# Two larger local units a batch, ScalarE score masks, GpSimd low bits and a new order in an attention + SoLU kernel

## The chip, the cores and the metric

The kernel runs on one core of a Trainium2 chip. That core has five engines with queues of their own: TensorE (PE in the profile, with PEld for its weight loads), VectorE (DVE), ScalarE (ACT), GpSimd (POOL) and SyncE (SP, which here only issues DMAs). The metric is the device time of one execution in microseconds (us). Three runs of the kernel before gave 503.68, 504.58 and 505.04; their median is 504.58.

## The reference

Eight batches of eight heads of attention over 576 positions with head dimension 64, and a feed-forward layer over the 4608 resulting tokens. Heads 0 to 3 see a local window of 32 positions, heads 4 to 7 see earlier positions with the same remainder modulo 32.

```python
scores = scale * np.matmul(q, k.transpose(0, 1, 3, 2))
rel = pos[:, None] - pos[None, :]
mask_local = (rel >= 0) & (rel < stride)                                  # stride = 32
mask_strided = (rel >= 0) & (pos[None, :] % stride == pos[:, None] % stride)
masks = np.stack([mask_local if h < H // 2 else mask_strided for h in range(H)], axis=0)
scores = np.where(masks[None], scores, -1e9)
attn = np.exp(scores - np.max(scores, axis=-1, keepdims=True))
attn = attn / (np.sum(attn, axis=-1, keepdims=True) + 1e-09)
x = np.matmul(attn, v)                       # then tokens by (heads x dim) = 4608 x 512
h = x @ w_in                                 # 512 -> 1024
e = np.exp(h - np.max(h, axis=-1, keepdims=True))
solu = h * (e / (np.sum(e, axis=-1, keepdims=True) + 1e-09))
mu = np.mean(solu, axis=-1, keepdims=True)
var = np.mean((solu - mu) ** 2, axis=-1, keepdims=True)
out = ((solu - mu) / np.sqrt(var + 1e-06) * g_ln) @ w_out                  # 1024 -> 512
```

The two weight matrices come as float64: the kernel is handed them as 64-bit words.

## The kernel before

**Numbers.** Products that need more than 16 bits are made of three float16 matmuls: a value is split in a high half and a low half (high x high, high x low, low x high). So each of weights, probabilities, attention outputs and layer activations has a step on ACT that writes the high half and one on DVE that writes the remainder.

**Units.** A batch's attention is cut into five units (`UNITS`): two strided ones of 6 and 5 blocks of 54 x 54 (half 1), and three local ones of 3 blocks of 64 queries x 96 keys (half 0). A unit covers two pairs of heads, so it has 2 x 6 = 12 score tiles at most. Its steps: masks into the score banks `s_ps`; scores by TensorE (line 374); the maximum (L380, DVE); for most units subtraction (L390, DVE), exponential (L392, ACT) and sum (L393, DVE), and for the units of `BY_BLOCK` the exponential tile by tile on ACT with the sum accumulated (L385); the reciprocal (L397, L398); the division (L401, POOL); the two halves (L409 ACT, L410 DVE); a DMA transpose (L412); the product with v (L432 strided, L442 local, TensorE) into the banks `x_ps`; and its two halves (L461 ACT, L462 DVE) into the buffers `xl` and `xs`. There is one pair of score banks and one pair of value banks for all units.

**Masks.** The first six units have their masks written by TensorE: a product of a unit matrix with the mask (L369). From unit 6 on (`SEEDED`) ACT copies the mask into the score banks (L361) and TensorE adds the scores to it.

**Feed-forward.** `ff(n)` works on 128 tokens, 36 times. First layer: two halves of 12 matmuls of 512 columns (L505 to L507) into two of three banks `h_ps`; maximum, exponential, products and sums on DVE and ACT (L511 to L522); small statistics on POOL (L525 to L555); the two halves of the normalized result (L562, L563), a DMA transpose (L566; the last two blocks by parts, L570); second layer: two halves of 12 matmuls (L575 to L577) into `o_ps`, the scaling (L583) and the store (L584).

**Weights.** `decode` turns the 64-bit words into float32 on the chip: ACT makes the leading bits from the upper word (L603), DVE shifts the lower word to its top three bits (L606) and joins them to the rest (L607). Each of the eight pieces is 128 x 1024. `prep_w` does so for w_in, sums its squares by TensorE (L620, and the diagonal L624) to find a power-of-two scale, and splits it (L628, L629). `prep_o` does so for w_out; its squares are made by ACT (L639, eight of them), weighted by g on DVE (L644, L645), summed by `pow2_scale` on TensorE (L264), and the matrix is split by L651 and L652.

**Order.** `Plan.add` collects the steps with their planned length and what they read and write; `ORDER` is a list of step numbers, written out in the source, and the steps are issued in that order. Each engine works through its own steps in order, so a step that waits holds all later steps of its engine. SP's queue holds loads and transposes alike. The first layer's matmuls need the split w_in and the attention outputs of their 128 tokens; the second layer's need the split w_out and the transposed activations.

Of the kernel before, what the change touches and what calls it, by code (L numbers as in the profile page):

```python
# [37 lines left out]
NU = len(UNITS)  # L38
P_SCALE = 64.0
# [12 lines left out]
SEEDED = NU + 1  # L52
BY_BLOCK = (2, 3, 4, 7, 8, 9)
# [700 lines left out]
```

## Time and profile before

| | |
|---|---|
| median of the runs (503.68 to 505.04) | 504.58 us |
| profiled execution | 503.42 us |
| its span, first to last instruction | 501.7 us |
| TensorE busy | 464.5 us, 93% |
| VectorE busy | 353.7 us, 71% |
| ScalarE busy | 364.9 us, 73% |
| GpSimd busy | 158.3 us, 32% |
| mean granted TensorE clock | 0.952 |

A row of the groups reads: line, engine, operation, out<-in with partitions x elements and type, count | busy us, mean ns of one | idle of the engine before them and what ended it. A row of the timeline or of the chain begins with its start and its length in us. In the slices each digit stands for a fortieth of the span, in tenths.

### The profile page before, as it was taken

The numbers are of one execution on the slowest core, as the hardware profiler recorded it, in microseconds if no ns is written. First come the engines' busy times: TensorE is split into PE (matmuls) and PEld (weight loads), VectorE is DVE, ScalarE is ACT, GpSimd is POOL, SyncE is SP. The second block draws the span as 40 slices with busy tenths as digits, with TensorE's granted clock in tenths as the row PEclk, the third lists the DMA queues.
The fourth block names the chain that finished last, engine by engine and source line by source line (L and its number), as shares of the span: only waits on it lengthen the run. The fifth ranks groups of instructions, "written<-read, shape, count | busy, mean of one in ns | idle before, by whom it ended". The sixth has DMA issues, their size and how long they took to land.

```text
span 501.7 us, 12430 instructions
## 1 busy us (share of the span) xinstructions
PE 464.5 (93%) x5049; PEld 240.7 (48%) x5049; DVE 353.7 (71%) x740; ACT 364.9 (73%) x647; POOL 158.3 (32%) x312
## 2 busy tenths in 40 slices
PE   6263798999999999999999999999999999999996
PEld 5153444454554545554555554555454444444442
DVE  2999888678887687787788777787756684544440
ACT  3895999987996878787786867587667677366551
POOL 3210115371342442333244231334144116132230
PEclk8555799999999999999999999999999999999999
DMA  8999787299696689888899797629754569435443
GB/s 316 381 277 338 223 244 168 60 250 231 192 254 115 162 197 204 189 231 159 233 191 209 122 230 170 146 51 197 162 103 96 95 133 171 64 78 101 65 105 105
DMA packets 153817, 88.02 MB, mean 175 GB/s; under 512 B 139808, under 2 KB 140448, under 8 KB 153248
## 3 DMA queue, kind: packets, MB, share of 16 engines
q1 hardware_dynamic: 148576, 77.79, 68.6%
q10 hardware_dynamic: 5184, 9.44, 5.8%
q8 instruction: 39, 0.64, 0.5%
q14 instruction: 18, 0.15, 0.1%
HBM read 39.24 MB, written 9.44 MB: 97 GB/s over the span
## 4 chain that ended last, share of the span: by engine, by line
PE 73%; ACT 9%; DVE 7%; DMA 5%; POOL 3%; issue 2%; SPq 1%; ACTq 0%; DVEq 0%; POOLq 0%
PE o_ps L575 11%; PE h_ps L505 10%; PE o_ps L577 10%; PE o_ps L576 10%; PE h_ps L506 10%; PE h_ps L507 10%; PE s_ps L374 6%; DMA cc<-cc 3%; PE x_ps L442 2%; PE x_ps L432 2%; ACT t L385 2%; DMA k<-kstr 1%; DVE m L380 1%; ACT raw L515 1%; DMA raw<-vstr 1%
## 5 line engine op out<-in xcount | busy, mean ns | idle before, releaser
L575 PE MATMUL o_ps<-ohi,cc 128*128 128x512 f16 x272 | 103.4, 380 | 0.9 <-DMA cc<-cc 0.9
L577 PE MATMUL o_ps<-ohi,cc 128*128 128x512 f16 x272 | 103.1, 379 | 0.0
L576 PE MATMUL o_ps<-obuf,cc 128*128 128x512 f16 x272 | 103.1, 379 | 0.0
L401 POOL TENSOR_TENSOR t<-t,m 128x576 f32<-128x576 f32 (+2 forms) x40 | 50.2, 1258 | 89.8 <-DVE m L398 63.7
L511 DVE TENSOR_REDUCE st<-h_ps 128x1 f32<-128x512 f32 x70 | 47.5, 684 | 32.6 <-PE h_ps L507 32.6
L515 ACT ACTIVATE raw<-h_ps,st,vsc 128x512 f32<-128x512 f32 x62 | 47.9, 774 | 20.4 <-DVE st L513 19.4
L563 DVE SCALAR_TENSOR_TENSOR cc<-raw,st,cc 128x1024 f16<-128x1024 f32 (+1 forms) x38 | 46.4, 1224 | 20.9 <-ACT cc L562 20.7
L517 DVE SCALAR_TENSOR_TENSOR raw<-h_ps,raw 128x512 f32<-128x512 f32 x70 | 47.3, 684 | 18.5 <-ACT raw L515 17.9
L505 PE MATMUL h_ps<-w,xl 128*128 128x512 f16 x140 | 53.8, 384 | 0.7 <-DVE raw L517 0.7
L506 PE MATMUL h_ps<-w,xl 128*128 128x512 f16 x140 | 53.4, 381 | 0.0
L507 PE MATMUL h_ps<-w,xl 128*128 128x512 f16 x140 | 53.3, 381 | 0.0
L505 PE MATMUL h_ps<-w,xs 128*128 128x512 f16 x140 | 53.1, 379 | 0.0
L506 PE MATMUL h_ps<-w,xs 128*128 128x512 f16 x140 | 53.1, 379 | 0.0
L507 PE MATMUL h_ps<-w,xs 128*128 128x512 f16 x140 | 53.1, 379 | 0.0
L521 ACT ACTIVATE raw<-raw,st 128x1024 f32<-128x1024 f32 x36 | 41.3, 1148 | 15.6 <-DVE st L520 15.2
L380 DVE TENSOR_REDUCE m<-s_ps 128x6 f32<-128x576 f32 (+2 forms) x40 | 30.4, 761 | 29.0 <-PE s_ps L374 27.9
L562 ACT ACTIVATE cc<-raw,st 128x1024 f16<-128x1024 f32 (+1 forms) x38 | 41.7, 1099 | 11.7 <-POOL st L552 8.9
L374 PE MATMUL s_ps<-k,q 64*54 64x54 f32 (+1 forms) x1280 | 45.7, 286 | 3.4 <-DMA k<-kstr 1.7
L374 PEld LDWEIGHTS s_ps<-k,q 64*54 64x54 f32 (+1 forms) x1280 | 40.0, 201 | 14.4 <-issue 7.1
L577 PEld LDWEIGHTS <-cc 128*128 128x128 f16 x288 | 28.2, 98 | 34.5 <-DMA cc<-cc 0.6
L575 PEld LDWEIGHTS <-cc 128*128 128x128 f16 x288 | 28.1, 98 | 33.5 <-DMA cc<-cc 2.0
L576 PEld LDWEIGHTS <-cc 128*128 128x128 f16 x288 | 28.2, 98 | 29.5
(149 smaller groups left out, 826.2 us busy)
## 6 DMA issues: line engine op xcount, KB each, us to landing
out<-ob ACTq DMA_DIRECT2D x36, 256.0 KB, 3.6
q<-qstr SPq DMA_DIRECT2D x8, 594.0 KB, 5.3
k<-kstr SPq DMA_DIRECT2D x8, 594.0 KB, 5.1
q<-qloc SPq DMA_DIRECT2D x8, 576.0 KB, 6.4
k<-kloc SPq DMA_DIRECT2D x8, 576.0 KB, 6.4
raw<-w_in SPq DMA_DIRECT2D x4, 1024.0 KB, 14.4
vrs<-vstr SPq DMA_DIRECT2D x5, 768.0 KB, 8.4
vrl<-vloc SPq DMA_DIRECT2D x5, 640.0 KB, 5.7
```

Source lines behind the costliest of these rows:

```text
L374: nc.tensor.matmul(s_ps[row : row + nq, pair, i * nk : (i + 1) * nk], q_raw[half][hs, q0 : q0 + (nq - 1) * nqb + 1 : nqb], k_raw[half][hs, ...
L401: add("pool", nx * nk / 520 + 0.03, lambda: nc.gpsimd.tensor_tensor(tv, tv, sm.unsqueeze(2).broadcast_to([P, nx, nk]), op=ALU.mult), r=TM, ...
L505: nc.tensor.matmul(hv[i], xhi[cc], whi[:, cc, cols], start=(cc == 0), stop=False)
L506: nc.tensor.matmul(hv[i], xhi[cc], wlo[:, cc, cols], start=False, stop=False)
L507: nc.tensor.matmul(hv[i], xlo[cc], whi[:, cc, cols], start=False, stop=(cc == 3))
L511: add("dve", 0.69, lambda i=i: nc.vector.tensor_reduce((nm, nm2)[i], hv[i], axis=AX.X, op=ALU.max, negate=True), r=[HH[i]], w=[(ST, "nm", i)])
L515: add("act", 0.73, lambda i=i, q=q: nc.scalar.activation(e[:, parts2[i]], hv[i], AF.Exp, bias=nm, scale=hs, accum_out=q), r=[HH[i], (ST, " ...
L517: add("dve", 0.7, lambda i=i, x=x: nc.vector.scalar_tensor_tensor(u[:, parts2[i]], hv[i], 1.0, e[:, parts2[i]], op0=ALU.mult, op1=ALU.mult ...
L563: add("dve", w / 980 + 0.23, lambda cols=cols: nc.vector.scalar_tensor_tensor(c[:, 1, cols], u[:, cols], r, c[:, 0, cols], op0=ALU.mult, o ...
L575: nc.tensor.matmul(o, ct[:, cc, :], ohi[:, cc, :], start=(cc == 0), stop=False)
L576: nc.tensor.matmul(o, ct[:, cc, :], olo[:, cc, :], start=False, stop=False)
L577: nc.tensor.matmul(o, ct[:, 8 + cc, :], ohi[:, cc, :], start=False, stop=(cc == 7))
```

## The change

- Batches 1 to 7 have two local units, of 5 and 4 blocks (`LATER`), in place of three of 3. Batch 0 keeps its three. A 5-block unit's values fill both banks of `x_ps`, one pair of heads in each; a 4-block unit's fill one. The buffers for scores, probabilities and transposes are now one for each kind of unit and sized for it.
- All masks are written by ACT; the strided one is read straight from the loaded mask. TensorE's mask matmuls are gone, and two early matmuls write the score banks once.
- `BY_BLOCK` holds units 2, 3, 4, 7 and 8.
- In `decode` POOL takes the top byte of the lower word and makes the three bits of it by an addition and a product that rounds to an integer; DVE only joins them.
- The sum of squares of w_out is made by TensorE from the top halves of the decoded weights, with a diagonal, and multiplied by the sum of squares of g.
- Forty warming matmuls of 128 columns become ten of 480, and the sums of squares of v go to a buffer of v's halves.
- `ORDER` is a new list of 1517 steps (1586 before).

```diff
+LATER = [(1, 0, 6), (1, 6, 5), (0, 0, 5), (0, 5, 4)]
-SEEDED = NU + 1
-BY_BLOCK = (2, 3, 4, 7, 8, 9)
+BY_BLOCK = (2, 3, 4, 7, 8)
...
-    t_sb = buf("t", [P, 12 * QS], n=NTB)
-    m_sb = buf("m", [P, 24], n=NTB + 1)
-    p_sb = buf("p", [P, 12, P], F16, n=NPB)
-    pt_sb = buf("pt", [P, 12, P], F16, n=NPT)
+    t_sb = [buf(f"t{j}", [P, w])[0] for j, w in enumerate((12 * QS, 10 * QS, 10 * KL, 8 * KL))]
+    m_sb = buf("m", [P, 24], n=5)
+    p_sb = [buf(f"p{j}", [P, w, P], F16)[0] for j, w in enumerate((12, 12, 20, 16))]
+    pt_sb = [buf(f"pt{j}", [P, w, P], F16)[0] for j, w in enumerate((20, 16))]
...
-    add("pe", 2.13, warm, r=["ones"], w=["o"])
+    add("pe", 0.4, lambda: warm(2, [s_ps[:, i, 0 : 5 * KL] for i in range(2)]), r=["ones"], w=[("s", 0), ("s", 1)])
+    add("pe", 2.0, lambda: warm(10, [o_ps[:, 0 : 5 * KL]]), r=["ones"], w=["o"])
+    add("dve", 0.1, lambda: nc.vector.memset(s_ps[:, 1, 504:512], 0.0), w=[("s", 1)])
...
     def unit(n):
         b, j = divmod(n, NU)
-        half, b0, nb = UNITS[j]
+        half, b0, nb = (LATER if b else UNITS)[j]
...
-        if n >= SEEDED:
-
-            def seed():
-                nc.scalar.copy(s_ps[:, :, 0 : nb * nk], mk.unsqueeze(1).broadcast_to([P, 2, nb * nk]))
-
-            add("act", nx * nk / 1200 + 0.17, seed, r=["mask"], w=[("s", 0), ("s", 1)])
+        if half:
+            mk, MK = mask_sb[:, 2:3, 0:QS].unsqueeze(1).broadcast_to([P, 2, nb, QS]), "mask_raw"
+        else:
+            mk, MK = mk_loc[:, 0 if b0 == 0 else 1, 0:nb].unsqueeze(1).broadcast_to([P, 2, nb, KL]), "mask"
+        add("act", nx * nk / 1200 + 0.17, lambda: nc.scalar.copy(sv, mk), r=[MK], w=[("s", 0), ("s", 1)])
...
-            for pair, h, hs, row in heads if n < SEEDED else ():
-                nc.tensor.matmul(s_ps[row : row + D, pair, 0 : nb * nk], unit_sb[hs, hs], mk[hs], start=True, stop=False)
...
-        nt = 12
+        nt = 12 if half else 2 * nx
...
+        one = half == 0 and nb <= 4
+        X = [("x", xb)] if one else [("x", 0), ("x", 1)]
...
-        def bits():
-            nc.vector.tensor_scalar(w0, w0, 29, None, op0=ALU.logical_shift_right)
-            nc.vector.scalar_tensor_tensor(di, di, 3, w0, op0=ALU.logical_shift_left, op1=ALU.bitwise_or)
-
-        add("dve", 2.02, bits, r=[*RAW, *w], w=[*w, *RAW], lock=True)
+        top = raw.bitcast(U8).rearrange("p f (t b) -> p f t b", b=4)[:, :, 0, 3]
+        add("pool", 1.05, lambda: nc.gpsimd.tensor_scalar(w0, top, -15.5, 1.0 / 32, op0=ALU.add, op1=ALU.mult), r=RAW, w=[("low", n)])
+        add("dve", 1.25, lambda: nc.vector.scalar_tensor_tensor(di, di, 3, w0, op0=ALU.logical_shift_left, op1=ALU.bitwise_or),
+            r=[*RAW, ("low", n), *w], w=[*w, *RAW], lock=True)
...
     def prep_o():
+        add("dve", 0.2, lambda: nc.vector.scalar_tensor_tensor(gs_sb, g_sb, 1.0, g_sb, op0=ALU.mult, op1=ALU.mult, accum_out=o_sc[:, 9:10]), r=["g"], w=["gm", "gs"])
...
-            for cc in (2 * i, 2 * i + 1):
-                add("act", 0.71, lambda cc=cc: nc.scalar.activation(ob_sb[cc % 2][:, 0 : DM // 2].bitcast(BF16), obuf[:, cc], AF.Square,
-                                                                   scale=2.0**-SQ, accum_out=o_sc[:, 8 + cc : 9 + cc]),
-                    r=[("od", cc)], w=[("om", cc), ("ob", cc % 2)])
-
-        def comb():
-            nc.vector.tensor_tensor(o_sc[:, 8:16], o_sc[:, 8:16], g_sb, op=ALU.mult)
-            nc.vector.tensor_tensor(o_sc[:, 8:16], o_sc[:, 8:16], g_sb, op=ALU.mult)
+            def gram(i=i, dst=dst):
+                x = dst.bitcast(BF16).rearrange("p (f t) -> p f t", t=2)[:, :, 1]
+                for j in range(8):
+                    nc.tensor.matmul(o_ps[:, 0:P], x[:, j * P : j * P + P], x[:, j * P : j * P + P], start=(i == 0 and j == 0), stop=(i == 3 and j == 7))
+
+            add("pe", 0.6, gram, r=OD, w=["o"])
+
+        add("dve", 0.3, lambda: nc.vector.scalar_tensor_tensor(diag, o_ps[:, 0:P], 1.0, unit_sb, op0=ALU.mult, op1=ALU.mult, accum_out=o_sc[:, 8:9]),
+            r=["o", "unit"], w=["om"])
...
-        for j in range(2, NU - 1):
+        last = len(LATER if b else UNITS) - 1
+        for j in range(2, last):
```

More of the change, by code (lines that the diff above doesn't have):

```diff
@@ L221, in attn_solu_kernel, with warm @@
     add("dve", 0.3, lambda: nc.vector.memset(ones, 1.0), w=["ones"])
-    def warm():
-        for _ in range(40):
-            nc.tensor.matmul(o_ps[:, 0:P], ones, ones, start=True, stop=True)
-    add("pe", 2.13, warm, r=["ones"], w=["o"])
+    def warm(n, out):
+        for i in range(n):
+            nc.tensor.matmul(out[i % len(out)], ones, ones[:, 0:1].broadcast_to([P, 5 * KL]), start=True, stop=True)
+    add("pe", 0.4, lambda: warm(2, [s_ps[:, i, 0 : 5 * KL] for i in range(2)]), r=["ones"], w=[("s", 0), ("s", 1)])
+    add("pe", 2.0, lambda: warm(10, [o_ps[:, 0 : 5 * KL]]), r=["ones"], w=["o"])
+    add("dve", 0.1, lambda: nc.vector.memset(s_ps[:, 1, 504:512], 0.0), w=[("s", 1)])
     def masks_bf16():
         m = mask_sb
-        nc.gpsimd.tensor_copy(mk_str, m[:, 2:3, 0:QS].broadcast_to([P, 6, QS]))
         nc.gpsimd.tensor_copy(mk_loc[:, 0, 0:1], m[:, 0:1])
-        nc.gpsimd.tensor_copy(mk_loc[:, 0, 1:3], m[:, 1:2].broadcast_to([P, 2, KL]))
-        nc.gpsimd.tensor_copy(mk_loc[:, 1], m[:, 1:2].broadcast_to([P, 3, KL]))
+        nc.gpsimd.tensor_copy(mk_loc[:, 0, 1:5], m[:, 1:2].broadcast_to([P, 4, KL]))
+        nc.gpsimd.tensor_copy(mk_loc[:, 1], m[:, 1:2].broadcast_to([P, 5, KL]))
     def load_masks():
         add("sp", 0.4, lambda: nc.sync.dma_start(mask_sb, masks), w=["mask_raw"])
-        add("pool", 1.34, masks_bf16, r=["mask_raw"], w=["mask"])
-    for i in range(NPB):
+        add("pool", 1.4, masks_bf16, r=["mask_raw"], w=["mask"])
+    for i in range(4):
         def pads(i=i):
-            nc.gpsimd.memset(p_sb[i][:, :, QS:D], 0.0)
-            nc.gpsimd.memset(p_sb[i][:, :, D if i == 1 else KL : P], 0.0)
-        add("pool", 0.56, pads, w=[("p", i)])
+            if i < 2:
+                nc.gpsimd.memset(p_sb[i][:, :, QS:D], 0.0)
+            nc.gpsimd.memset(p_sb[i][:, :, (KL, D)[i == 1] : P], 0.0)
+        add("pool", (0.56, 0.9, 0.6, 0.5)[i], pads, w=[("p", i)])
     def unit_matrix():
@@ L262, in total @@
             for i, part in enumerate(parts):
-                nc.tensor.matmul(tot, ones, part.bitcast(BF16)[:, 1:2], start=(i == 0 and not adds), stop=(i == len(parts) - 1), skip_group_check=adds)
+                one = product or not (i or adds)
+                nc.tensor.matmul(tot[:, i : i + 1] if product else tot, ones, part.bitcast(BF16)[:, 1:2], start=one, stop=product or i == len(parts) - 1, skip_group_check=adds)
         add("pe", 0.06 * len(parts) + 0.05, total, r=["ones", *r], w=[T])
         def root():
-            nc.vector.tensor_scalar(dst[:, 0:1].bitcast(I32), tot.bitcast(I32), 1, 0x7F800000, op0=ALU.logical_shift_right, op1=ALU.bitwise_and)
+            low = tot
+            if product:
+                low = dst[:, 0:1]
+                nc.vector.tensor_scalar(low, tot[:, 0:1], tot[:, 1:2], None, op0=ALU.mult)
+            nc.vector.tensor_scalar(dst[:, 0:1].bitcast(I32), low.bitcast(I32), 1, 0x7F800000, op0=ALU.logical_shift_right, op1=ALU.bitwise_and)
         def fn():
@@ L278, in fn @@
                 nc.vector.tensor_scalar(dst[:, 2:3], dst[:, 1:2], dst[:, 1:2], square, op0=ALU.mult, op1=ALU.mult)
-        add("dve", 0.16, root, r=[T], w=[(w, "root")])
+        add("dve", 0.32 if product else 0.16, root, r=[T], w=[(w, "root")])
         add("dve", 0.54, fn, r=[(w, "root")], w=[w])
@@ L300, in v_scale @@
         raw = raw_v(b)
+        junk = v_sb[1][b % 2]
         for a in range(2):
             def square(a=a):
-                nc.scalar.activation(junk[:, 0 : VW[a]], vr_sb[raw][a], AF.Square, scale=2.0**-SQ, accum_out=vm[:, a : a + 1])
-            add("act", (1.36, 1.58)[a], square, r=[("vr", a, raw)], w=["junk", ("vm", b % 2, a)])
+                nc.scalar.activation(junk[:, a, 0 : VW[a]], vr_sb[raw][a], AF.Square, scale=2.0**-SQ, accum_out=vm[:, a : a + 1])
+            add("act", (1.36, 1.58)[a], square, r=[("vr", a, raw)], w=[("v", 1, b % 2, a), ("vm", b % 2, a)])
         room = (s_ps[:, 1, 512 - b : 513 - b], ("s", 1)) if b else (h_ps[2][:, 0:1], ("h", 2))
-        pow2_scale(sc, [vm[:, 0:1], vm[:, 1:2]], [("vm", b % 2, a) for a in range(2)], ("vsc", b % 4), room, 8, 1.0 / P_SCALE, adds=b > 1)
+        pow2_scale(sc, [vm[:, 0:1], vm[:, 1:2]], [("vm", b % 2, a) for a in range(2)], ("vsc", b % 4), room, 8, 1.0 / P_SCALE, adds=b > 0)
         def hscale():
@@ L374, in qk @@
                     nc.tensor.matmul(s_ps[row : row + nq, pair, i * nk : (i + 1) * nk], q_raw[half][hs, q0 : q0 + (nq - 1) * nqb + 1 : nqb],
-                                     k_raw[half][hs, k0 : k0 + nk], start=False, stop=(i == nb - 1), skip_group_check=n >= SEEDED)
-        add("pe", nb * 0.231 + (0.25, 0.09)[half] - (0.2 if n >= SEEDED else 0.0), qk, r=[("q", half), ("k", half), "mask", "unit", "kpad"], w=[("s", 0), ("s", 1)])
+                                     k_raw[half][hs, k0 : k0 + nk], start=False, stop=(i == nb - 1), skip_group_check=True)
+        add("pe", nb * 0.231 + (0.25, 0.09)[half] - 0.2, qk, r=[("q", half), ("k", half), "kpad"], w=[("s", 0), ("s", 1)])
         SS = [("s", 0), ("s", 1)]
@@ L404, in unit @@
         if half == 0:
-            hi, lo = (pb[:, 6 * a : 6 * a + 6, 0:nk] for a in range(2))
+            hi, lo = (pb[:, nx * a : nx * a + nx, 0:nk] for a in range(2))
         else:
@@ L438, in pv @@
                     vv, vb = (v_sb[0][0] if blk % 2 else ve_sb), (blk + 1) // 2
-                    for a, (vp, pp) in enumerate((vv[0:nk, a], ptb[0:nk, y + x]) for a, y in ((0, 0), (0, 6), (1, 0))):
+                    for a, (vp, pp) in enumerate((vv[0:nk, a], ptb[0:nk, y + x]) for a, y in ((0, 0), (0, nx), (1, 0))):
                         for h in range(2):
                             v0 = (vb * 4 + 2 * pair + h) * D
-                            nc.tensor.matmul(x_ps[xb][h * D : (h + 1) * D, x * nq : (x + 1) * nq], vp[:, v0 : v0 + D], pp[:, (h ^ pair) * QL : (h ^ pair) * QL + nq],
+                            nc.tensor.matmul(x_ps[xb if one else pair][h * D : (h + 1) * D, (x if one else i) * nq : ((x if one else i) + 1) * nq], vp[:, v0 : v0 + D], pp[:, (h ^ pair) * QL : (h ^ pair) * QL + nq],
                                              start=(a == 0), stop=(a == 2))
@@ L449, in unit @@
             q0, w = off + QL * b0, QL * nb
-            src = [x_ps[xb][:, 0 : 2 * w].rearrange("p (c q) -> p c q", c=2)]
-            dst = [[x[:, :, q0 : q0 + w] for x in xl]]
+            src = [x_ps[xb][:, 0 : 2 * w].rearrange("p (c q) -> p c q", c=2)] if one else [x[:, 0:w] for x in x_ps]
+            dst = [[x[:, :, q0 : q0 + w] for x in xl]] if one else [[x[:, c, q0 : q0 + w] for x in xl] for c in range(2)]
             ring = [("xl", q0 // QL + i) for i in range(nb)]
@@ L458, in unit @@
         for c, (src, (dh, dl)) in enumerate(zip(src, dst)):
-            w = 2 * by_row[c] * nq if half else nx * nq
-            K = [(*x, c) if half else x for x in ring]
+            w = 2 * by_row[c] * nq if half else (2 if one else 1) * nb * nq
+            K = [(*x, y) for x in ring for y in (range(2) if one else (c,))]
             add("act", w / 1200 + 0.17, lambda src=src, dh=dh: nc.scalar.copy(dh, src), r=[X[c]], w=[(*x, "h") for x in K])
@@ L479, in ff @@
         bs = sorted({n * P // S, (n * P + P - 1) // S})
-        ring = [("xl", pos // QL + i, a) for i in range(2) for a in "hl"]
+        ring = [("xl", pos // QL + i, c, a) for i in range(2) for c in range(2) for a in "hl"]
         ring += [("xs", b % 2, b0, c, a) for b in bs for b0 in R0 for c in range(2) for a in "hl"]
@@ L681, in attn_solu_kernel @@
                 o_factor(b + 1)
-        unit(b * NU + NU - 1)
+        unit(b * NU + last)
         if b == 0:
```

43 lines of the change are left out of this document (16 added, 27 removed), and 78 rows, old and new, of the table ORDER.

## The prediction

> **What bounds the kernel now.** I read the page's slices first. In them TensorE (PE) is thin for the first eighth of the span and full from then on; the granted clock is a half in that first part.
>
> ```profile
> PE   6263798999999999999999999999999999999996
> PEclk8555799999999999999999999999999999999999
> ```
>
> The timeline dates the change: VectorE (DVE) and ScalarE (ACT) begin near 9.3 us, the first feed-forward (ff) matmul at 55.8, the first of the second layer at 79.5.
>
> ```profile
> 9.23 1.27 ACT L303 ACTIVATE junk<-vrl 128x1280 bf16<-128x1280 f32 x1 [7.17 <-DMA vrl<-vloc]
> ...
> 55.79 0.61 PE L505 MATMUL h_ps<-w,xl 128*128 128x512 f16 x1
> ...
> 79.48 0.39 PE L575 MATMUL o_ps<-ohi,cc 128*128 128x512 f16 x1 [0.89 <-DMA cc<-cc]
> ```
>
> Then the busy time by stage. The columns are the stretch, its length, then the busy time of PE, PEld, DVE, ACT, GpSimd (POOL), then PEclk and the DMA share.
>
> ```profile
> 9.30:62.00 52.70, 25.40 (x543) 19.33 (x543) 48.78 (x88) 43.78 (x98) 7.72 (x7) 0.55 1.02 311
> 30.00:40.00 10.00, 4.98 (x136) 4.59 (x140) 9.03 (x27) 9.96 (x25) 2.26 (x3) 0.50 1.07 285
> 40.00:50.00 10.00, 3.18 (x101) 2.86 (x96) 9.37 (x9) 4.76 (x6) 1.15 (x1) 0.50 1.16 342
> 62.00:100.00 38.00, 35.12 (x367) 16.95 (x366) 30.37 (x73) 36.11 (x86) 13.64 (x27) 1.00 0.64 161
> 100.00:498.00 398.00, 397.58 (x4051) 198.71 (x4049) 274.28 (x578) 282.99 (x463) 133.09 (x264) 1.00 0.73 157
> ```
>
> So there are two kernels in one. Up to 62 us DVE sets the pace: 48.8 of 52.7 us busy, against 43.8 for ACT, a PE that mostly waits, and an idle POOL. From 62 to 100 PE is nearly full and ACT too (36.1 of 38). After 100 us PE sets it alone: 0.4 us of 398 idle, DVE at 69%, ACT at 71%. Work taken off DVE counts in the first part; in the second only what shortens PE's own stream counts. The chain of waits shows the same: before 62 us it runs through DVE's decoding of the weights, later through PE steps without a gap.
>
> ```profile
> 48.17 0.61 DVE raw L606
> ...
> 48.87 1.24 DVE obuf L607
> ...
> 50.13 0.72 ACT ob L639 x2
> ```
>
> **The change, startup part.** These are the groups of the first 64 us that it touches.
>
> ```profile
> L606 DVE TENSOR_SCALAR raw<-raw 128x1024 int32<-128x1024 int32 x7 | 4.8, 685 | 0.0
> L624 DVE SCALAR_TENSOR_TENSOR diag<-h_ps,unit 128x128 bf16<-128x128 f32 x1 | 0.3, 292 | 0.5 <-PE h_ps L620 0.5
> L639 ACT ACTIVATE ob<-obuf 128x512 bf16<-128x512 f32 x8 | 5.0, 627 | 3.9 <-DVE obuf L607 3.8
> L361 ACT CAST s_ps<-mk_loc 128x576 f32<-128x576 bf16 x1 | 0.6, 639 | 0.0
> L620 PE MATMUL h_ps<-cc 128*128 128x128 bf16 x32 | 4.1, 305 | 3.3 <-DVE cc L607 3.3
> L232 POOL CAST mk_loc<-mask 128x96 bf16<-128x96 f32 x1 | 0.3, 270 | 0.0
> L234 POOL CAST mk_loc<-mask 128x288 bf16<-128x288 f32 x1 | 0.4, 432 | 0.0
> L401 POOL TENSOR_TENSOR t<-t,m 128x576 f32<-128x576 f32 (+2 forms) x7 | 8.5, 1227 | 47.9 <-DVE m L398 28.6 <-ACT xl L461 14.3 <-DVE o_sc L644 5.0
> ```
>
> *DVE.* Eight shifts of L606 (seven in this group, one on the other staging tile) leave it: 8 x 0.685 = -5.5 us. Two small products (L644, L645) go, and a small operation in the root and the squares of g come: they cancel. New is a diagonal like L624 with the read of its accumulator: +0.4. In batch 1 three local units become two. A reduction of the same kind took 0.828 us for 648 elements and 0.715 for 540, so 1.05 ns an element:
>
> ```profile
> L380 DVE TENSOR_REDUCE m<-s_ps 128x12 f32<-128x648 f32 x8 | 6.6, 828 | 10.9 <-PE s_ps L374 10.9
> L380 DVE TENSOR_REDUCE m<-s_ps 128x10 f32<-128x540 f32 x8 | 5.7, 715 | 1.5 <-PE s_ps L374 1.5
> L380 DVE TENSOR_REDUCE m<-s_ps 128x6 f32<-128x576 f32 x24 | 18.1, 754 | 16.6 <-PE s_ps L374 15.5 <-ACT raw L521 1.1
> L397 DVE TENSOR_SCALAR m<-m 128x6 f32<-128x6 f32 x24 | 4.7, 195 | 0.1
> ```
>
> By that slope units of 960 and 768 elements take 1.16 + 0.96 instead of 3 x 0.754, -0.14 for the maximum and as much for the low half, and three small operations of one unit, 0.19 each like L397, go: -0.9. In sum DVE loses 6.0 us before the first second-layer matmul.
>
> *ACT.* Eight squares go, 0.72 each in the chain above (two of them, cut, in the row; 0.63 plus the accumulator's read in the group): -5.8. Six units that PE seeded with the masks are now seeded by ACT: one of 0.71, one of 0.61, three of 0.64 and one of 0.71, scaled from L361: +4.0. Net -1.9. ACT had 8.9 us idle between 9.3 and 62, so with a window 6.0 shorter and 1.9 less work it keeps 4.8. It also begins earlier: its first operation waited until 9.23 for v, which the new order loads ahead of q and k. So it is no bound, but nearly one.
>
> *POOL.* It gets the eight masks, as one operation with one input of 1024 elements. The casts give 0.84 ns an element over 0.19 us, so 1.05 us; from above, L401 with two inputs gives 1.227/576 = 2.13 ns, 2.2 us. I take 1.05, the row with one input. POOL was idle for 45 of these 53 us, so its own time hides. Behind each mask on POOL's queue stands the next unit's L401; a mask that waits for its weights' DMA would hold that too, but weights 0 are loaded before the local q and k in the new order.
>
> The Trainium skill, GPSIMD Engine Reference, 4.1 Engine selection, says one-input elementwise work there is roughly at line rate; an estimate from its 1.03 cycles an element at 1.2 GHz is 0.88 us plus dispatch, and the term would not change by it.
>
> What does not hide is that POOL and DVE get in each other's way. The same operation of DVE, with two inputs from SBUF, took 1.80 us at 19.09 and 2.38 at 40.38, where it met an L401:
>
> ```profile
> 19.09 1.80 DVE L326 SCALAR_TENSOR_TENSOR vs<-vrs,vsc,vs 128x1536 f16<-128x1536 f32 x1
> ...
> 40.00 1.15 POOL L401 TENSOR_TENSOR t<-t,m 128x576 f32<-128x576 f32 x1 [7.02 <-DVE m L398]
> 40.38 2.38 DVE L326 SCALAR_TENSOR_TENSOR vs<-vrs,vsc,vs 128x1536 f16<-128x1536 f32 x1 [0.55 <-ACT vs L325]
> ```
>
> The overlap was 0.77 us and DVE lost 0.58. Half of DVE's startup work is of that kind (L326, L410, L607, L629). If every second mask meets it for half its length, 8 x 0.5 x 0.5 x 0.58/0.77 = 1.5; part of this is a wait that L606 would have caused as DVE work. I charge +1.0, with 0 and 8.4 (all masks waited out) as ends.
>
> The Trainium skill, SBUF — State Buffer, section "SBUF: two separate sides", states it harder: the pair of ports is an exclusive lock and the loser blocks for the whole instruction. By it the 40.38 operation would have ended at 41.15 + 1.80 = 42.95; it ended at 42.76, so the trace nearly agrees, and a DVE that always lost would pay 8.4 us, which is the slower rival below.
>
> *PE and order.* The sums of squares of w_out add 32 matmuls like L620, four groups of 1.03 us at half clock, 0.5 at full. Two groups now stand behind the first ff half, in PE's queue ahead of the second: +1.0. The 24 mask matmuls (L369) go, off the path. The new order loads v first and q, k after: DVE's first large operation comes near 11.5 us instead of 9.26, but the scaling of v, some 2.5 us of DVE, is then already done; I count zero. The DMA share is 1.16 at 40 to 50 us, and w_out waits for staging rooms as before: +1.0 for that and for ACT, with 0 and 4 as ends. Startup: -6.0 + 1.0 + 1.0 + 1.0 = -3.0 us; ends -6 and +5.
>
> **The change, PE-bound part.** All ff matmuls stay. What changes is how often PE is interrupted by attention. The chain gives each such visit; a steady ff step is 0.22, the step after a visit 0.32:
>
> ```profile
> 126.70 0.22 PE h_ps L506
> ...
> 145.56 1.18 PE s_ps L374 x40
> ...
> 155.40 0.88 PE s_ps L374 x24
> ...
> 158.98 0.69 PE x_ps L442 x36
> 159.66 0.32 PE o_ps L575
> ...
> 164.95 1.26 PE x_ps L442 x72
> ...
> 186.36 0.70 PE x_ps L432 x72
> ...
> 189.76 1.39 PE s_ps L374 x48
> 191.15 0.32 PE h_ps L505
> ...
> 283.16 0.70 PE x_ps L432 x72
> 283.86 1.34 PE s_ps L374 x48
> 285.20 0.32 PE h_ps L505
> ```
>
> A lone local unit costs 0.88 + 0.10 for its scores and 0.69 + 0.10 for its values. Scores of 40 and 48 matmuls differ by 0.21, 0.026 a matmul; on that slope 40 and 32 local ones cost 1.30 + 1.09 + 0.20 = 2.59 against 3 x 0.98 = 2.94, -0.35. Were all of 0.88 proportional, 1.47 + 1.17 + 0.20, only -0.10. Values: 36 more matmuls cost 0.57, so 60 and 48 take 1.07 + 0.88 + 0.20 = 2.15 against 2.37: -0.22. A batch saves 0.32 to 0.57; seven batches 2.2 to 4.0; I take 3.1. Visits joined save a switch: the pair at 283.16 cost 0.70 + 1.34 + 0.10 = 2.14, the two alone 0.80 + 1.49 = 2.29, so 0.15. After the first second-layer matmul the old order has 57 visits with 14 joints, the new one 37 with 21: 7 more, -1.0 (0 to -1.5). The small remainder of batch 1 that the new order has yet to do is +0.1. Part two: -4.0, ends -2.2 and -5.5. The rest (DVE, ACT, transposes with 20 + 16 tiles for 3 x 12) is hidden under that full PE while DVE and ACT have 30% free; without it nothing of it would exceed the 0.8 us a batch counted above, in the good direction.
>
> **Sum.** The profiled execution took 503.42 us (span 501.7 and 1.7 around it). 503.42 - 3.0 - 4.0 = 496.4. The median of the runs, 504.58, stands 1.2 above the profiled one, so 497.6.
>
> **Rivals.**
> 1. *ACT or the loads take DVE's place in the startup.* ACT's work falls by 1.9 only, and from 30 to 40 us it is busy 9.96 of 10, and from 62 on it is full; against it stand its idle half at 40 to 50 and its earlier start. Startup then gains 0 to 1.9, and the time is 504.6 - 4.0 - 1 = 499.6.
> 2. *Larger units stall PE.* One unit of 5 blocks keeps the score banks for 0.97 + 1.4 + 1.16 + 1.15 us and needs both value banks, so a score visit can find them unready. For it: the score banks exist once. Against it: PE waited 0.4 us in 398, and four large units keep the banks no longer than five small ones. At 0.6 us a batch, 7 x 0.6 = 4.2, part two is gone: 501.7.
> 3. *Slower: GpSimd and DVE exclude each other in the startup.* Place: the eight masks, each between the landing of weights and DVE's L607. Price: at 2.2 us a mask and a DVE that waits it out, 17.6 instead of the 1.0 charged: 497.6 + 16.6 = 514; with half of it covered by DVE work from PSUM, 505.4; middle 510. It decides from (504.6 - 497.6 + 1.0)/8 = 1.0 us of DVE wait a mask, the whole of my 1.05.
> 4. *No change:* part one returns nothing and the new order, with ACT full between 62 and 100, adds 3.4 us of idle PE to the 2.9 there: 504.6 - 4.0 + 3.4 = 504.
>
> **How the numbers follow.** Forecast 0.60 (493 to 501), rival 1 0.15, rival 2 0.10, rival 3 0.09, rival 4 0.06. About 0.3%, 1.5 us, is what a measurement tells from no change. Faster: 0.60 + 0.15 + 0.09 of rival 2 = 0.84; same: rival 4 and the rest of rival 2, 0.07; slower 0.09. The range runs from 504.6 - 6 - 5.5 = 493 to 503, which takes in rivals 1 and 2 and leaves rivals 3 and 4 and a tail of the forecast out.
>
> **What would show it.** Right: DVE's masks gone and POOL's about 1.05 us each; the first ff matmul near 51 us, the first second-layer one near 76.5; 37 visits after it, local scores of 40 matmuls near 1.3 us; PE from there to its end 4 us shorter. Wrong: POOL masks over 2 us and L607, L629 or L410 stretched beside them; ACT full while DVE idles before the first ff matmul; PE idle by more than 2 us after 100 us with a release by s_ps seeds or x_ps copies.

## Result and profile after: slower, with less work on every engine that mattered

The changed kernel takes 507.46 us (median of 12 executions, 505.43 to 510.96) against 504.96 for the kernel before in the same sessions: a ratio of 1.0053, 95% interval 1.003 to 1.0076. It was forecast at 497.6 and came out slower by 0.5%; the interval begins at the 0.3% that can be told apart. The profiled execution took 505.71 us (span 504.0), 2.3 more than that of before.

The timeline of TensorE in the changed kernel (start, duration, engine, line) has the first feed-forward (ff) matmul 1.2 us earlier than before, and the first of the second layer 2.1 us later. Line numbers are those of the changed kernel, two or three below those of before.

```profile
54.61 0.61 PE L503 MATMUL h_ps<-w,xl 128*128 128x512 f16 x1
...
81.60 0.39 PE L573 MATMUL o_ps<-ohi,cc 128*128 128x512 f16 x1 [0.22 <-DMA cc<-cc]
...
499.90 0.38 PE L575 MATMUL h_ps<-ohi,cc 128*128 128x512 f16 x1
```

Stretches of the prediction, columns as there (PE, PEld, DVE, ACT, POOL, PEclk, DMA share, and last GB/s):

```profile
9.30:62.00 52.70, 29.86 (x586) 22.17 (x586) 42.76 (x76) 39.26 (x79) 21.54 (x19) 0.64 1.04 317
62.00:100.00 38.00, 33.21 (x435) 16.98 (x434) 31.36 (x75) 35.28 (x88) 13.65 (x25) 1.00 0.78 190
100.00:498.00 398.00, 393.88 (x3994) 198.74 (x3992) 273.96 (x543) 280.12 (x444) 132.64 (x259) 1.00 0.71 153
```

VectorE lost 6.0 us of work before 62 us (48.78 to 42.76), ScalarE 4.5. That the first equals the 6.0 that was worked out is partly luck, since other steps now fall into the stretch: over the first 100 us VectorE lost 4.9 (79.44 to 74.50). The freed time stayed empty: VectorE is busy for 81% of the stretch instead of 93%. From 62 to 100 us TensorE idles 1.9 us more than before, from 100 to 498 us 3.7 us more (4.1 of 398, it was 0.4).

The cleanest account is TensorE from its first to its last ff matmul. Before:

```profile
55.79:498.02 442.23, 438.93 (x4476) 218.53 (x4472) 310.45 (x662) 324.67 (x565) 147.95 (x291) 1.00 0.72 157
```

After:

```profile
54.61:500.28 445.67, 436.56 (x4509) 220.64 (x4506) 311.09 (x626) 319.86 (x539) 148.68 (x285) 1.00 0.72 158
```

So: start -1.2, work -2.4 (438.93 to 436.56; two groups of the new sums of squares now lie in this stretch), idle +5.8 (3.30 to 9.11), together +2.3, the whole difference. The waits of TensorE in that stretch, by releaser (total us, times, longest):

```profile
PE o_ps L573 <- DMA cc<-cc: 3.1, 4, 1.8
PE h_ps L503 <- DVE raw L515: 2.2, 3, 1.5
PE o_ps L573 <- ACT s_ps L364: 1.4, 1, 1.4
PE h_ps L573 <- DMA cc<-cc: 1.2, 1, 1.2
```

The largest, 4.3 of 9.1 us, is the DMA transposition of the second layer's input (cc<-cc, median 4.7 us from issue to landing) that landed late; the 4.1 us of idle time behind 100 us are all of this kind. The row that names ScalarE's score seed (s_ps L364) may be one more: its wait ended at 94.90, and the transposition for that matmul, issued at 88.25, had landed only at 94.77. The chain of waits of the changed kernel shows three late transpositions between 100 and 480 us, two of them below, and, in the startup, three transfers that hold 23.5 us of the chain between 9 and 62 us. In the kernel before that chain ran over VectorE and ScalarE alone until 59.9.

```profile
26.78 8.05 DMA pt<-p
...
39.41 6.30 DMA raw<-w_out
...
50.21 9.15 DMA q<-qloc
...
152.48 8.03 DMA cc<-cc
...
299.84 9.66 DMA cc<-cc
```

The GpSimd operation on the low bits (L606; the prediction calls it a mask) behaves as costed where it is alone, and not where it meets VectorE. Groups of the changed kernel:

```profile
L606 POOL TENSOR_SCALAR raw<-raw 128x1024 int32<-128x1024 uint8 x7 | 10.7, 1525 | 16.0 <-DMA raw<-w_out 12.8 <-DMA raw<-w_in 3.1
L606 POOL TENSOR_SCALAR cc<-cc 128x1024 int32<-128x1024 uint8 x1 | 1.1, 1135 | 2.1 <-DVE m L379 2.1
L650 DVE TENSOR_SCALAR gs<-g,o_sc 128x8 f32<-128x8 f32 x1 | 1.6, 1603 | 0.0
```

The timeline shows whom it meets. A join of VectorE (L607, which joins the low bits to the rest) keeps its 1.22 us, and the GpSimd operation beside it takes 2.07. Later a tiny VectorE product of eight columns, 0.22 us before, takes 1.60 beside a GpSimd division that now has 960 elements.

```profile
15.07 1.22 DVE L607 SCALAR_TENSOR_TENSOR cc<-cc,raw 128x1024 int32<-128x1024 int32 x1
15.27 2.07 POOL L606 TENSOR_SCALAR raw<-raw 128x1024 int32<-128x1024 uint8 x1
...
66.49 1.79 POOL L400 TENSOR_TENSOR t<-t,m 128x960 f32<-128x960 f32 x1 [0.96 <-DVE o_sc L276]
66.71 1.60 DVE L650 TENSOR_SCALAR gs<-g,o_sc 128x8 f32<-128x8 f32 x1
```

That product gates the first scaled second-layer weight on ScalarE. The Trainium skill, SBUF — State Buffer, section "SBUF: two separate sides", says that whoever starts first holds the shared pair of ports and the other blocks for the whole instruction; both pairs of rows agree: the GpSimd operation ends 1.05 us behind the join (alone it takes 1.09 to 1.14), and the product ends within 0.03 us of the division.

### The profile page after: what moved, and what is told of

It is laid out like the page before. It is cut to its first block, busy times and chain, and to the rows that moved or that the text cites. A ratio compares the mean times of both kernels' runs of the same rounds, so it can differ in the third digit from the quotient of the medians.

```text
span 504.0 us, 12300 instructions
## 1 busy us (share of the span) xinstructions
PE 460.2 (91%) x5023; PEld 239.0 (47%) x5023; DVE 348.5 (69%) x695; ACT 359.6 (71%) x617; POOL 170.3 (34%) x312
## 4 chain that ended last, share of the span: by engine, by line
PE 71%; DMA 12%; ACT 8%; DVE 3%; issue 2%; POOL 1%; SPq 1%; ACTq 0%; POOLq 0%; DVEq 0%
PE o_ps L573 11%; PE o_ps L574 10%; PE o_ps L575 10%; PE h_ps L503 10%; PE h_ps L504 9%; PE h_ps L505 9%; PE s_ps L373 5%; DMA cc<-cc 5%; DMA pt<-p 3%; PE x_ps L440 2%; DMA q<-qloc 2%; PE x_ps L430 2%; ACT t L384 2%; DMA raw<-w_out 1%; ACT vs L307 1%
## 5 line engine op out<-in xcount | busy, mean ns | idle before, releaser
L400 POOL TENSOR_TENSOR t<-t,m 128x648 f32<-128x648 f32 (+4 forms) x33 | 47.3, 1434 | 99.7 <-DVE m L397 63.2
L561 DVE SCALAR_TENSOR_TENSOR cc<-raw,st,cc 128x1024 f16<-128x1024 f32 (+1 forms) x38 | 47.5, 1251 | 21.9 <-ACT cc L560 21.6
L373 PE MATMUL s_ps<-k,q 64*54 64x54 f32 (+1 forms) x1280 | 44.1, 284 | 12.6 <-ACT s_ps L364 12.4
L373 PEld LDWEIGHTS s_ps<-k,q 64*54 64x54 f32 (+1 forms) x1280 | 38.9, 201 | 20.9 <-ACT s_ps L364 15.5
L581 ACT ACTIVATE ob<-o_ps,st 128x512 f32<-128x512 f32 x34 | 23.3, 684 | 30.1 <-PE o_ps L575 15.9
```

The source lines that it names most:

```text
L373: nc.tensor.matmul(s_ps[row : row + nq, pair, i * nk : (i + 1) * nk], q_raw[half][hs, q0 : q0 + (nq - 1) * nqb + 1 : nqb], k_raw[half][hs, ...
L400: add("pool", nx * nk / 520 + 0.03, lambda: nc.gpsimd.tensor_tensor(tv, tv, sm.unsqueeze(2).broadcast_to([P, nx, nk]), op=ALU.mult), r=TM, ...
L561: add("dve", w / 980 + 0.23, lambda cols=cols: nc.vector.scalar_tensor_tensor(c[:, 1, cols], u[:, cols], r, c[:, 0, cols], op0=ALU.mult, o ...
```

## Experiments

Five readings of these profiles were set against each other. *Theory 1*: the startup is bound by the DMA engines (98.8% busy in the first 60 us before, 100.1% after), so VectorE's saving buys nothing. *Theory 2*: GpSimd and VectorE exclude each other, so the operations themselves give the gain back. *Theory 3*: the saving of VectorE is real and only the new order brings transfers into the chain. *Theory 4*, formed from the account of TensorE: the operations are worth what was predicted, and the complete order that came with them loses it again by idle TensorE; *theory 5* is its rival, that such gaps only show where the engines are late, and come back elsewhere.

### One part alone: low bits on GpSimd in the kernel before

```diff
-            nc.vector.tensor_scalar(w0, w0, 29, None, op0=ALU.logical_shift_right)
+        # in the step of the Prelu:
+            nc.gpsimd.tensor_scalar(w0, top, -15.5, 1.0 / 32, op0=ALU.add, op1=ALU.mult)
```

> The kernel before, its order unchanged, with only the low three bits of the weights moved to GpSimd (the shift of L606 becomes a GpSimd operation on the top byte, issued right behind the Prelu). Prediction's step: DVE bounds the startup, so eight shifts of 0.62 to 0.68 us less bring -4.5 us (498.5 to 501 on the median), first second-layer matmul near 75. Theory 1 (the DMA engines, busy 98.8% of 0 to 60 us, bound the startup under any order): -1 to 0 us, that matmul within 1 us of 79.5. Theory 2 (GpSimd and VectorE exclude each other, so the moved work comes back as waits): 0 to +2 us, the GpSimd operation at 1.8 us and more where a two-input VectorE operation runs. Theory 3 (only the new order brings the transfers into the chain, the DVE saving is real): -3 to -5 us.

Measured: 506.46 us, ratio 1.0032 (1.0017 to 1.0047), slower; the first second-layer matmul came at 82.25. VectorE's busy time in the startup fell by 1.5 us only, from 48.78, although 5.5 us of shifts are gone (lines of this run's own kernel):

```profile
9.30:62.00 52.70, 23.55 (x505) 17.59 (x500) 47.30 (x75) 42.48 (x92) 20.94 (x14) 0.74 0.99 310
```

The rest went into longer operations. The four joins of w_in take 1.68 us each where they took 1.23, as the group shows,

```profile
L612 DVE SCALAR_TENSOR_TENSOR cc<-cc,raw 128x1024 int32<-128x1024 int32 x4 | 6.6, 1682 | 0.0
```

and in the timeline two low halves (L410) of 576 elements take 1.64 to 1.66 where they took 0.75:

```profile
46.67 1.20 POOL L607 TENSOR_SCALAR raw<-raw 128x1024 int32<-128x1024 uint8 x1 [0.85 <-DMA raw<-w_out]
46.82 1.66 DVE L410 TENSOR_TENSOR p<-t,p 128x576 f16<-128x576 f32 x1
...
50.57 1.21 POOL L607 TENSOR_SCALAR cc<-cc 128x1024 int32<-128x1024 uint8 x1 [2.71 <-PE s_ps L374]
50.73 1.64 DVE L410 TENSOR_TENSOR p<-t,p 128x576 f16<-128x576 f32 x1
```

So theory 2 describes this kernel. Under an order not made for it the moved work comes back as longer operations: of the 5.5 us taken away, VectorE's busy time in this stretch kept 4.0, 1.8 of it in the four joins and 1.8 in the two low halves. Theory 3 as stated falls.

### The same part undone in the changed kernel

```diff
-        add("pool", 1.05, lambda: nc.gpsimd.tensor_scalar(w0, top, -15.5, 1.0 / 32, ...), ...)
+        add("pool", 1.05, lambda: None, r=RAW, w=[("low", n)])
+            nc.vector.tensor_scalar(w0, w0, 29, None, op0=ALU.logical_shift_right)   # ahead of the join
```

> The changed kernel with its own order, low three bits back on VectorE (shift and join, as before). Prediction's step: +4.5 us. Theory 1 and theory 3 (in the changed kernel the chain of 0 to 62 us runs over transfers, VectorE has room): 0 to +1.5 us, first second-layer matmul 81.6 to 83. Theory 2 (exclusion costs what was gained): -1 to -2 us.

Measured: 509.86 us, ratio 1.0099 (1.0078 to 1.012): 2.4 us above the changed kernel, first second-layer matmul at 83.33. Under the new order the low bits on GpSimd do help, by half of the 4.5 charged. (The profiled execution also ran 3.4 us at half rate near 311 us, of which below; how much of the 2.4 this is stays open.) Theory 2 alone cannot be the loss.

### Fewer bytes

```diff
-        load(1.49, q_raw[half][:, 0:w], (qloc, qstr)[half][b], [("q", half)])
+        load(1.49, q_raw[half][:, 0:w], (qloc, qstr)[half][b], [("q", half)], skip=b == 1)   # keys, values too
```

> The kernel before without the six loads of batch 1 (queries, keys and values of batch 1 are not read; batch 1 is computed from batch 0's), 3.8 MB less in the startup. Theory 1: several us faster, -3 us or more at the first second-layer matmul (79.5). Theory 3: its chain of 9 to 60 us runs over VectorE and ScalarE alone, so 0 to -1 us. Theory 2: nothing to say of it.

> The changed kernel without the six loads of batch 1 (batch 1 is computed from batch 0's queries, keys and values). Theory 1 and theory 3: its chain holds 23.5 us of transfers by 62 us, so the first second-layer matmul comes 3 to 6 us earlier than 81.6 and the time is 501 to 504. Theory 2: no change, 507.

Batch 1 is then computed from batch 0's inputs, so only the time of these runs is of use. Measured: 504.77 us without these loads in the kernel before, ratio 1.0001 (0.9991 to 1.0011); 507.63 in the changed one, 1.0046 (1.0017 to 1.0076). The first 60 us of the first move 14.9 MB instead of 18.8, and the busy share of the queue in the DMA view falls from 98.8% to

```profile
q1 hardware_dynamic: 10896, 14.84, 81.7%
```

and nothing comes earlier for it. The first second-layer matmul comes at 80.60, against 79.48 with all loads; in the changed kernel it comes at 81.50, against 81.60. Theory 1 falls in both kernels; a queue that is always busy was no bound. In the changed kernel without these loads one transposition still landed 10.69 us after its issue at 41.48; two of w_out's loads stood ahead of it.

### Repairing single places of the new order

The first run moved four steps; the lines below give one of these moves in words. A tile is a block of 128 tokens, and "two moves" are two DMA copies on the chip (ve<-vl).

```diff
-  ... load v (batch 7), two moves, transposition of tile 17 ...
+  ... transposition of tile 17, load v (batch 7), two moves ...
```

> The changed kernel with four places of its order moved and nothing else: the second-layer transposition of tile 17 goes ahead of the load and the two moves that stood in front of it in SP's queue (landing 9.66 us after its issue at 299.84, TensorE idle 1.84 us at 309.55), that of tile 6 ahead of one load (8.03 us at 152.48, idle 0.87 at 160.55), and the last tile's transpositions are issued as soon as each quarter is written (idle 1.22 at 494.92). Theory 4 (the changed kernel loses by idle TensorE between its matmuls, 9.10 us behind the first feed-forward matmul against 3.27 before, and these places are of the order, not of the new operations): the three gaps go, idle 5.5 to 7, time 3 us less, 503.5 to 505. Theory 5 (the gaps only show where the other engines are late, and come back elsewhere): 506.5 to 508, idle 8.5 or more.

Measured: 507.29 us, ratio 1.0054 (1.0036 to 1.0071), no gain. The tail's gap is gone and the wait at 160 us too, but at 310 us the gap came back longer, with another releaser: the squares of v of batch 7, one of whose loads now stands behind the transposition. In all TensorE idles 7.7 us from its first ff matmul on (9.1 in the changed kernel), between the two ranges that were expected. That first matmul came at 56.70, 2.1 us later, though nothing was moved ahead of it: so much can two profiles of one startup differ. And after 3.4 us of idleness TensorE's steps take 0.43 us instead of 0.22 until 314.7:

```profile
310.82 0.19 PE L263 MATMUL s_ps<-vm,ones 128*128 128x1 bf16 x2 [3.40 <-ACT vs L307]
...
311.69 0.63 PE L573 MATMUL o_ps<-ohi,cc 128*128 128x512 f16 x1
...
314.93 0.38 PE L575 MATMUL o_ps<-ohi,cc 128*128 128x512 f16 x1
```

The granted clock of 312 to 318 us is 0.77 there, against 1.00 in the changed kernel's own trace, where the idleness was 1.83. The Trainium skill, TensorE: Matmul & The Clock Gate, Part 1, puts the fall to half rate behind a window of about 3.4 us without work; the 3.40 us here agree, other traces of nearly the same order don't. The kernel with fewer loads fell behind 2.99 us (0.81 in the same stretch), the second run of this section behind 2.24, and the one with the low bits on VectorE behind 1.95:

```profile
310.35 0.39 PE L573 MATMUL o_ps<-ohi,cc 128*128 128x512 f16 x1 [1.95 <-DMA cc<-cc]
...
312.57 0.63 PE L575 MATMUL o_ps<-ohi,cc 128*128 128x512 f16 x1
```

The third run of this section did not fall behind 2.81 us (clock 1.00):

```profile
311.27 0.39 PE L573 MATMUL o_ps<-ohi,cc 128*128 128x512 f16 x1 [2.81 <-DMA cc<-cc]
```

So the length of one idle time does not decide it in these traces. Theory 5 holds for this place: the order around 300 us is too tight for that move.

```diff
-  ... load w_out 0, load w_out 2, a move, transposition of unit 2 ...
+  ... a move, transposition of unit 2, load w_out 0, load w_out 2 ...
```

> The changed kernel with two of the four loads of w_out issued behind the transposition of unit 2 instead of ahead of it (that transposition, issued at 41.54, landed only near 52.5, and ScalarE idled 3.16 us for it). If the order of the SP queue makes the start late: that transposition lands within 6 us, first feed-forward matmul 51 to 53 instead of 54.6. If w_out's own path to the scaled second-layer weights sets the first second-layer matmul, that one stays at 81.6 or comes up to 3 us later; if ScalarE's idle time between 50 and 62 us sets it, it comes 1 to 3 us earlier. Time 505 to 508.

Measured: 512.58 us, ratio 1.0154 (1.0128 to 1.018); first ff matmul at 59.59, five later. The sums of squares of w_out stand in TensorE's queue ahead of the scores and values that the first ff matmul needs, and they now waited for the late weights:

```profile
54.00 1.89 PE L643 MATMUL o_ps<-obuf 128*128 128x128 bf16 x16 [7.62 <-DVE obuf L607]
```

A third run moved a single step: it put the ten matmuls on ones behind the scores of unit 5, so that TensorE would be at full rate for the first ff matmuls.

> The changed kernel with one step moved: the ten matmuls on ones (at 11.74 us in its profile) go behind the scores of unit 5 (45 us). If the half rate of the first eight feed-forward matmuls (0.43 us instead of 0.2157, 54.61 to 57.57) comes from TensorE's idleness before them, they run at the full rate and the time falls by 0.5 to 2 us; if the start is bound by ScalarE behind 62 us anyway, the matmuls are faster and the time stays within 1 us of 507.

Measured: 509.44 us, 1.0093 (1.0059 to 1.0126). The first six ff matmuls still took some 0.42 us a step (55.20 to 57.71); another wait of 2.33 us stood between. The gap at 311 us was 2.81 us. It doesn't answer its question.

### The order as a whole

The next kernels keep every operation and replace only the text of ORDER. Two complete orders come from one sum: each step starts when its engine is free and what it reads is there, with the durations noted at the steps, and single steps are moved until the end is early.

```diff
 ORDER = """
-10 6 1 15 8 16 9 13 11 14 20 25 17 18 53 30 52 54 19 2 55 35 12 4 56 60 58 5 61 59 3 21 22 62 123 63 7 23 76 64 77 26 27 65 92 66 78 67 79 93 97 80 98
+(another order of the same steps)
```

> All new operations of the change under another complete order, found by moving single steps of the changed kernel's order so that the end, as worked out from the durations noted at the steps (the scores 0.225 us dearer, as the traces show), is early for early and for late transfers alike (1.9, 2.6 and 3.4 us from queue to landing). Theory 4: TensorE idle behind the first feed-forward matmul under 5 us, time 497 to 502. Theory 2 (GpSimd and VectorE exclude each other, a cost of the operations themselves): 504 or more under any order.

> The kernel before under an order found in the same way from its own. By the same sum the new operations are worth 3.7 us between the two orders so found. Theory 4: 499 to 504, so 2 to 5 us above the changed kernel's contents under their order. Theory 2: the two within 1 us, or this one faster.

Measured: 506.39 us for the new operations (1.0036, 1.0012 to 1.0061), 505.17 for the old (1.0005, 0.9994 to 1.0016). By these numbers it is theory 2's ranges that are met. But its reason isn't in the trace of the first: that one begins its ff matmuls at 50.74, 3.9 us earlier than the changed kernel and at full rate, and then loses 11 us of idle TensorE (under 5 were expected), half of it in one wait:

```profile
50.74 0.39 PE L503 MATMUL h_ps<-w,xl 128*128 128x512 f16 x1
...
95.73 0.58 PE L573 MATMUL o_ps<-ohi,cc 128*128 128x512 f16 x1 [5.26 <-DMA cc<-cc]
```

That transposition was issued at 85.33 and landed 10.27 us later, behind two other transpositions, two moves and a load. The sum had given transpositions the noted durations. So it was fitted to the first and last ff matmul of six measured kernels, with transpositions 1.5 to 1.9 times as long as noted, an issue that blocks SP while the queue is full, and 4 us of half rate after more than 2.5 us of idle TensorE. These are settings of the sum and not measurements: the idle times above do not bear out the 2.5.

> All new operations of the change under a third order. The sum behind it is fitted to six runs measured so far (first and last feed-forward matmul of each): transpositions take 1.5 to 1.9 times the noted duration in the queues, SP's issue of one blocks while the queue before it is full, TensorE runs at half rate for 4 us after more than 2.5 us of idleness. Theory 4 (order, not operations): TensorE idle behind the first feed-forward matmul under 5 us against 9.1, last matmul 491 to 495, time 496 to 500, faster than both kernels. Theory 2 (operations themselves cost the gain): 503 or more.

> All new operations of the change under a fourth order from the same fitted sum, searched from the changed kernel's own order with another seed. Theory 4: 496 to 501; a spread of more than 4 us between this and the other order of the same sum would say that the sum, not the operations, is what is short.

> The kernel before under an order from the same fitted sum. By that sum its last matmul comes 5 to 7 us behind that of the changed operations under theirs: 497 to 500, time 502 to 505. Theory 4: that difference is the worth of the operations, about what was predicted for the whole change (-7 us). Theory 2: the two within 2 us.

> The operations of the kernel before under a second order from the fitted sum (last matmul at 496.3 in the sum, against 491.3 for the new operations). If the worth of the operations is what the first pair showed (498.61 against 505.10): 502 to 506. If that pair was a lucky draw of orders: 500 or less.

| operations | order | us | ratio to before (95%) |
|---|---|---|---|
| new | fitted, first | 498.61 | 0.9878 (0.9855 to 0.990) |
| new | fitted, second | 503.68 | 0.9967 (0.9945 to 0.9988) |
| new | of the change | 507.46 | 1.0053 (1.003 to 1.0076) |
| old | of the kernel before | 504.96 | 1 |
| old | fitted, first | 505.10 | 1.0001 (0.9983 to 1.0019) |
| old | fitted, second | 506.62 | 1.0044 (1.0029 to 1.0059) |

The first is faster than both kernels, by 6.4 us against before, within 1.0 us of the forecast. Its rows: the ff matmuls begin at 48.15, 6.5 us earlier than in the changed kernel, and TensorE idles 0.35 us of the 393 behind 100 us.

```profile
48.15 0.61 PE L503 MATMUL h_ps<-w,xl 128*128 128x512 f16 x1
```

```profile
48.15:492.68 444.53, 438.09 (x4525) 221.42 (x4522) 317.37 (x635) 323.00 (x542) 161.72 (x289) 1.00 0.76 163
100.00:492.60 392.60, 392.25 (x3946) 196.51 (x3943) 271.14 (x533) 277.33 (x443) 141.24 (x264) 1.00 0.74 154
```

Against before it starts 7.6 us earlier, works 0.8 less and idles 3.1 more; 5.8 of its 6.4 us of idle time (under 5 were expected) lie before 82 us. The forecast had 3.0 for the startup and 4.0 behind it, so the nearness of the totals is partly luck. Its first second-layer matmul comes at 83.21, later than in either kernel: TensorE had other work. In its SP queue the transpositions of batch 0's first four units stand ahead of the loads of w_out:

```profile
41.16 1.62 SPq L411 DMA_TRANSPOSE pt<-p  x1
42.89 1.37 SPq L288 DMA_DIRECT2D raw<-w_out  x2
```

The median landing of its second-layer transpositions is 5.4 us, later than the 4.7 of the changed kernel, and no matmul waits for one. What differs, it seems, is the room that the order leaves them. Theory 4 is borne out: the best order of the new operations is 6 us faster than the best of the old ones, and four orders of the same operations lie 9 us apart. How much the operations are worth in general is less sure. In pairs of one search the new ones gain 6.5 us (first fitted), 2.9 (second fitted), and lose 1.2 (not fitted). The two fitted orders of the new operations are 5 us apart as well, so the sum behind them is short too; 503.68 and 506.62 lie above the ranges expected for them. One thing holds for all three searches: the first ff matmul comes at 48.15 to 50.74 with the new operations and at 56.68 to 58.04 with the old ones.

### Which operations carry it

> The fastest order so far (498.61 us with the new operations), unchanged, with the low three bits back on VectorE. The prediction's step makes the moved shifts worth 4.5 us (5.5 of VectorE less 1.0 of waits): 502.5 to 503.5. If the waits of GpSimd and VectorE for each other eat most of it, as in the kernel before with the bits on GpSimd: 498 to 500.

Measured: 501.70 us, ratio 0.9951 (0.9934 to 0.9967): the low bits on GpSimd are worth 3.1 us under that order (3.7 by the ratios, since the kernel before, run beside it, was 0.5 us faster than beside the others). The first ff matmul comes 1.2 us later with them on VectorE, and TensorE idles 8.0 us from first to last instead of 6.4:

```profile
49.39:496.06 446.67, 438.66 (x4525) 221.40 (x4522) 320.15 (x639) 323.37 (x542) 157.44 (x285) 1.00 0.75 163
```

> All new operations except the larger units: every batch keeps local units of 3, 3 and 3 blocks, under an order of its own from the same fitted sum (which puts it within 1 us of the larger units). If the larger units carry the gain of TensorE's visits (4.6 us in the traces, 4.0 predicted): 502 to 505. If the rest carries it: 498 to 501.

```diff
-LATER = [(1, 0, 6), (1, 6, 5), (0, 0, 5), (0, 5, 4)]
+LATER = UNITS
```

Measured: 508.89 us, 1.0093 (1.0074 to 1.0113), worse than predicted by either reading. From its first to its last ff matmul TensorE is busy 446.29 us, 8.2 more than with the larger units, but part of it is at half rate (granted clock 0.81 at 62 to 80 us, 0.91 at 80 to 100; an estimate from these two is at most 5.2 us of the 8.2):

```profile
47.79:503.47 455.68, 446.29 (x4562) 224.56 (x4558) 322.30 (x672) 325.96 (x551) 153.27 (x295) 0.99 0.76 162
```

Its order is its own, and orders of one sum differ by 5 us, so the worth of the larger units by themselves stays open here; what speaks for them is the count of TensorE's steps, below. The first ff matmul came at 47.79 without the larger units and at 49.39 without the low bits on GpSimd, so neither of the two carries the early start of the searched orders. Which of the other operations does was not tested.

## Why the prediction was wrong

*DVE sets the pace up to 62 us, -6.0.* The amount was about right, the conclusion drawn from it was not. That DVE set the pace, busy for 48.8 of 52.7 us, was true of one order. With 5.5 us taken away the old order gave 4.0 back in longer operations beside GpSimd; the new one left VectorE idle behind transfers. This is the first step that failed: for the startup -3.0 was forecast, +2.1 came. Its two terms of +1.0, for collisions and for loads and ScalarE, were too small. Of the 5.5 us of shifts the time got back 3.1 under the best order, 2.4 under the order of the change and none under the old one. Which wait holds the startup of the changed kernel stays open: without six loads, or with two loads of w_out moved, it was no faster, and only another complete order was. The end of +5 for the startup did hold the result, but the range did not use it: 504.6 + 5 - 2.2 is 507, and the range stopped at 503. The ends of the terms themselves would give -5 (-6 and 1.0) and +7.4 (-6, 8.4, 1.0 and 4).

*POOL at 1.05 us a mask.* Right alone (1.09 to 1.14), 1.5 to 2.1 where it meets VectorE. In the changed kernel it is mostly GpSimd that pays, since VectorE's operations began first.

*The date of the first second-layer matmul* was a poor mark. The fastest kernel has it at 83.2. What counts is when TensorE's steady work begins and how long it idles in all.

*PE-bound part, -4.0.* The work was right. From the first second-layer matmul on, all time between starts of ff matmuls beyond 0.2157 us, less idle time, is 61.1 us before and 56.7 after: -4.4 (gaps above 0.3 us; all gaps give -4.6). But its idle time went from 1.7 to 6.5, and for that the step had charged nothing ("DVE and ACT have 30% free"). This is the second step that failed. Of the 6.5 us, 4.1 are waits for late transpositions, 1.4 the wait at 94.9 for a transposition or a score seed, and 0.9 a wait for ScalarE's squares of v. Free engines don't make a late transposition land; the order decides what stands ahead of it in the queue.

*The rivals.* Rival 4, that the order itself adds idle TensorE, had the mechanism; it allowed 3.4 us more between 62 and 100, measured are 5.8, 3.7 of them behind 100 us, and with the startup returning nothing its time was 504. It had 0.06. Rival 2's sign (idle TensorE behind 100 us by more than 2 us) appeared with other releasers, transpositions instead of score seeds and value copies. A score seed is named for one wait only, the 1.4 us at 94.9. Rival 1's place, the loads, is in the chain, but fewer bytes changed nothing. Rival 3 is true of the old order, at +1.7 us instead of the 510 it was priced at.

One point stays open: the changed kernel's median lies 1.8 us over its profiled execution. Five traces of its order with small edits show the wait near 310 us at 1.95 to 3.40 us instead of 1.83, with 3.4 us of half rate behind it in four of them. The mean granted clock was 0.963 in the two shortest executions of the changed kernel and 0.956 to 0.960 in the five above 509 us, which such a stretch would give (an estimate: 3.4 us at half rate take 0.003 off the mean). Where those executions lost it was not seen in a trace.

## What to carry to other kernels

A change that comes with a complete new order is two changes: judge the operations by counting work, and the order by where each engine's queue leaves late transfers no room; run the operations under several orders before calling them slow. An engine that is 93% busy, or a DMA queue that is 99% busy, is a bound only if taking work from it moves the next milestone, which one cheap experiment tells. Single repairs of this tight order moved the gap and did not close it.

## What the hardware showed unexpectedly

- A VectorE product over eight columns took 1.60 us instead of 0.22 beside a GpSimd operation of 1.79 us: here the price of meeting was what was left of the other operation, not its own length.
- The issue of one second-layer transposition on SP took 1.3 us at best, 2.0 in the median of the changed kernel, 3.0 in that of the fastest and up to 9.2 (units of 3); what stood behind it in SP's queue was issued later. From issue to landing it took from 4.2 us to 10.3 (first searched order) and 14.4 (units of 3).
- Idle time of TensorE in mid-kernel was followed by half rate behind 1.95, 2.24, 2.99 and 3.40 us (3.4 us each) and behind 5.26 us (95.7 to 99.9), and was not behind 1.83 and 2.81. Behind 3.40 us the half rate lasted from 311.3 to 314.7, so such a wait costs some 1.7 us more than it shows.
